# Reordering the head values by column tiles, masking keys per half, a float32 first piece of w_in, and another order of matmuls in block 1

## The chip, the cores and the metric

The kernel runs on one core of a Trainium2 chip. A core has five engines that work through their own instruction lists in order: TensorE (PE, matmuls; PEld are its weight loads), VectorE (DVE), ScalarE (ACT), GpSimd (POOL) and SyncE (SP, here only a queue that issues transfers). 16 DMA engines move data between device memory and the core's memory. The metric is device time in microseconds (us) of one execution; the median of several runs is compared.

## What is computed

Inputs are q, k, v of shape 8 x 8 x 576 x 64 (batch, heads, sequence, head width) and two weight matrices, all float32. The first stage is attention without softmax, with a decay per head, and causal; the second is a two-layer network with a hard-swish gate.

```python
scores = scale * np.matmul(q, k.transpose(0, 1, 3, 2))
gamma = 1.0 - 2.0 ** (-5.0 - np.arange(H, dtype=np.float32))
Dmat = np.where(rel >= 0, gamma[:, None, None] ** rel[None, :, :], 0.0)
attn = np.matmul(scores * Dmat[None], v)
x = attn.transpose(0, 2, 1, 3).reshape(B * S, H * D)      # 4608 x 512
h = x @ w_in                                               # 512 -> 2048
g = h * np.clip(h + 3.0, 0.0, 6.0) / 6.0
out = g @ w_out                                            # 2048 -> 512
```

## The kernel before

**Tokens and blocks.** Each of the 8 batches has 576 positions: a *head* of 64 (`TL`) and 512 (`BLK`) more. The heads of all batches together make block 0, 512 tokens; blocks 1 to 8 are the 512 later positions of each batch, in four chunks of 128 (`NCB`). Chunk number c counts from 4, so block 1 has chunks 4 to 7. There are 9 blocks (`NB`).

**Attention of a chunk.** Keys, queries and values come by SyncE's queue in float32 (`load`, L166), are cast and scaled (`casts`, L182: keys on ScalarE, queries and values on POOL) and turned on PE (`transposes`, L198; letters `c` and `t` of the plan below). Scores (`a`), products of keys and values (`s`), running state (`u`: VectorE L313 and L316, POOL L317), its cast to float16 (`z`, ScalarE L323 to L326), state times query (`x`) and scores times values (`i`) follow. The last writes PSUM, from where ScalarE copies xT, the transposed x of the block (L369).

**The network.** An up unit (`up_steps`, L491; letters L, R for the left and right half of a block's columns, U for both) makes one 128-wide slice of h from xT and a piece of w_in with four matmul steps; ScalarE makes u (L510), VectorE the gate product g (L512). Blocks 0 and 1 multiply g with w_out plainly (`down_plain`, L544; letter D is one step, 64 in a block); later blocks use a Strassen scheme, for which VectorE subtracts quarters of w_out (`weight_sums`, L644, instruction L527; letter `+`).

**Order.** Every engine's list is written by hand: the code emits instructions in the order of the function calls, and a plan string is read by `go` (L692). The tile framework adds the waits: an instruction waits on a semaphore for what it reads or overwrites.

**The heads, block 0.** The 64 head positions of a pair of batches lie as 4 (`NJ`) neighbouring positions per partition, 16 rows (`RP`) a batch. Keys and queries of head pair i are loaded in two halves (`load_half`, L390; keys of pairs 1 to 3 and all values by POOL's queue, which casts to float16 while it moves), cast on VectorE (`cast_heads`, L410) and turned on PE (`turn_heads`, L415, with the permutation `by_chunk`). Values are brought into the chunk's order by `values_heads` (L445): for each chunk four accumulated products with a sparse selection matrix `pick`, which is cleared by a POOL memset (L741) and filled by VectorE (`picks`, L431). Scores (L467) are multiplied with a mask `ws[3]` (L470), `inner_heads` (L473) multiplies them with the values and writes xT of block 0.

**The states that the heads leave.** `keys_heads` (L453) turns the head keys back on PE (hpk) and scales them by a decay on ScalarE (L458) into `kn`, which lies in the place of `ws[1]`. `head_states` (L271) multiplies `kn` with the values `vh` (in `ws[4]`) for each of four chunks; each chunk holds two batches in the two halves of its 128 rows, and each half's product is made by 64 x 64 quadrants of PE. In the plan these are `k0` to `k3` and `h0` to `h3`.

**Weights.** w_in is cut into four pieces of 512 columns, w_out into four of 512 rows; POOL's queue loads and casts them (L658, L663), after the keys and values of the heads. Up units 0 to 3 of block 0 need piece 0 of w_in, units 4 to 7 piece 1, and so on. SyncE's queue goes on with the chunks behind the third piece of w_out (`fetch(8, wout[2])`, L794).

## Time and profile before

| | us |
|---|---|
| median of 3 runs | 299.4 (299.04 to 300.53) |
| the profiled execution | 301.02 |
| its span, first to last instruction | 299.3 |
| w_in first piece landed, first up unit of block 0 | 18.0, 18.06 |
| unit 4 of block 0 | 22.27 |
| first head state on PE | 37.56 |
| chunk 4's scores | 44.98 |
| chunk 6's scores | 54.77 |
| chunk 8's scores | 67.31 |

The span covers the instructions alone; what lies around it makes the difference to the execution's time. A line of a timeline gives start, length, engine, source line, operation, tile written, tiles read and size, the number of instructions merged into it, and in brackets how long the engine had been idle before it and for whom. A matmul of 512 columns counts as busy for some 0.38 us, though the next one starts 0.11 us later. DMA shares can exceed 1, as transfers on one engine overlap.

### The profile page before, as it was taken

What the parts mean: (1) busy time and instruction counts of PE and PEld (TensorE: products, weight loads), DVE (VectorE), ACT (ScalarE), POOL (GpSimd) and SP (SyncE); (2) the same over time, 40 slices, a digit from 0 to 9 for tenths busy, and PEclk for the clock granted to TensorE, in tenths of its full rate; (3) what the DMA queues carried; (4) which work ended last, traced back from release to release, by engine and by line L of the source; (5) the groups of instructions that cost most, each with busy time, mean ns of one, the idle gap of its engine ahead of it and who ended that gap; (6) DMA issues with size and microseconds to landing.
All of it is one profiled execution on the core that took longest, in us unless ns stands there. A gap on an engine that the chain in (4) does not pass through costs nothing.

```text
span 299.3 us, 12661 instructions
## 1 busy us (share of the span) xinstructions
PE 287.4 (96%) x5574; PEld 219.3 (73%) x5574; DVE 216.2 (72%) x388; ACT 193.9 (65%) x360; POOL 133.7 (45%) x170
## 2 busy tenths in 40 slices
PE   4999998999999999999999999999999999999995
PEld 2776644777556667888777878778778987778894
DVE  7749545669897778788967797688869776647654
ACT  3748854799866696686677577667766574565420
POOL 8971057526762920719631962386247003100510
PEclk9999999999999999999999999999999999999999
DMA  6999999998999999997999999999906100200114
GB/s 157 157 182 213 186 227 209 227 228 183 161 216 164 249 202 191 178 239 195 225 220 225 169 201 216 150 177 247 148 3 142 72 2 30 102 15 2 72 72 140
DMA packets 119542, 47.86 MB, mean 160 GB/s; under 512 B 92352, under 2 KB 114880, under 8 KB 119488
## 3 DMA queue, kind: packets, MB, share of 16 engines
q1 hardware_dynamic: 114336, 41.56, 71.1%
q0 software_dynamic: 4720, 5.11, 10.5%
q8 instruction: 43, 0.70, 1.0%
q10 hardware_dynamic: 432, 0.39, 0.5%
q14 instruction: 11, 0.09, 0.1%
HBM read 36.70 MB, written 9.44 MB: 154 GB/s over the span
## 4 chain that ended last, share of the span: by engine, by line
PE 79%; DMA 9%; POOL 6%; SPq 2%; ACT 2%; issue 1%; DVE 1%; POOLq 0%; ACTq 0%
PE ph L153 37%; PE pm L153 29%; DMA wout<-in_moe_w_out_dram 6%; PE pd L153 5%; PE po L231 4%; DMA fq<-in_q_dram 2%; PE pa L231 2%; SPq L174 2%; POOL hv L439 1%; POOL hk L399 1%; POOL win L658 1%; PE pu L231 1%; POOL ws L741 1%; PE ptk L153 1%; POOL q L192 1%
## 5 line engine op out<-in xcount | busy, mean ns | idle before, releaser
L153 PE MATMUL ph<-xT,win 128*64 128x512 f16 (+1 forms) x1248 | 144.8, 364 | 1.2 <-DMA win<-in_moe_w_in_dram 0.5
L512 DVE SCALAR_TENSOR_TENSOR g<-u,ph 128x512 f16<-128x512 f32 (+1 forms) x156 | 98.8, 643 | 53.1 <-ACT u L510 52.6
L510 ACT ACTIVATE u<-ph,half 128x512 f32<-128x512 f32 (+1 forms) x156 | 100.5, 659 | 43.0 <-PE ph L153 40.6
L153 PEld LDWEIGHTS <-win 128*64 128x64 f16 x1248 | 82.9, 136 | 28.6 <-DMA win<-in_moe_w_in_dram 1.1
L153 PEld LDWEIGHTS <-g 128*64 128x64 f16 x928 | 51.1, 110 | 14.9 <-issue 0.4
L153 PEld LDWEIGHTS <-s 128*64 128x64 f16 x896 | 50.3, 110 | 8.1 <-issue 0.2
L317 POOL TENSOR_TENSOR z<-z,gpow 128x256 f32<-128x256 f32 x24 | 15.8, 657 | 69.1 <-DVE z L316 51.2
L153 PE MATMUL pm<-ws,s 128*64 128x256 f16 x672 | 45.6, 273 | 0.0
L192 POOL TENSOR_TENSOR q<-fq,dec 128x512 f16<-128x512 f32 x32 | 36.7, 1166 | 3.4 <-DVE zh L282 1.7
L369 ACT CAST xT<-po 128x256 f16<-128x256 f32 (+1 forms) x44 | 22.5, 583 | 23.4 <-PE po L231 22.5
L195 POOL TENSOR_TENSOR v<-fv,dec 128x512 f16<-128x512 f32 x32 | 35.4, 1111 | 2.1 <-DMA fv<-in_v_dram 2.1
L591 POOL TENSOR_TENSOR u<-u,p 128x512 f32<-128x512 f32 x7 | 8.9, 1271 | 60.4 <-ACT u L631 54.2
L153 PE MATMUL pd<-wout,g 128*64 128x512 f16 x256 | 34.7, 382 | 0.1
L153 PE MATMUL pm<-wout,g 128*64 128x256 f16 x448 | 31.1, 273 | 0.0
L266 DVE TENSOR_TENSOR a<-pa,mask 128x256 f16<-128x256 f32 (+1 forms) x44 | 21.9, 539 | 8.4 <-PE pa L231 4.7
L188 ACT CAST k<-fk 128x512 f16<-128x512 f32 x32 | 19.9, 622 | 2.1 <-DMA fk<-in_k_dram 2.1
L527 DVE TENSOR_TENSOR s<-g 128x1024 f16<-128x1024 f16 x28 | 19.3, 692 | 0.2
L323 ACT CAST z<-z 128x512 f16<-128x512 f32 x24 | 14.9, 622 | 5.1 <-DVE z L313 4.7
L153 PE MATMUL pm<-ws,g 128*64 128x256 f16 x224 | 16.7, 274 | 0.0
L153 PE MATMUL pm<-wout,s 128*64 128x256 f16 x224 | 16.3, 273 | 0.1
L527 DVE TENSOR_TENSOR s<-g,s 128x1024 f16<-128x1024 f16 x14 | 13.3, 949 | 0.0
L231 PE MATMUL po<-qT,z 64*64 64x64 f16 x512 | 12.5, 198 | 0.4 <-ACT z L326 0.3
(106 smaller groups left out, 270.0 us busy)
## 6 DMA issues: line engine op xcount, KB each, us to landing
fk<-in_k_dram SPq DMA_DIRECT2D x32, 256.0 KB, 4.6
fq<-in_q_dram SPq DMA_DIRECT2D x16, 512.0 KB, 6.0
fv<-in_v_dram SPq DMA_DIRECT2D x32, 256.0 KB, 5.5
out_dram<-o SPq DMA_DIRECT2D x14, 512.0 KB, 3.8
wout<-in_moe_w_out_dram POOLq DMA_DIRECT2D x4, 512.0 KB, 17.9
out_dram<-o SPq DMA_DIRECT2D x7, 256.0 KB, 5.4
win<-in_moe_w_in_dram POOLq DMA_DIRECT2D x3, 512.0 KB, 10.9
hq<-in_q_dram SPq DMA_DIRECT2D x6, 128.0 KB, 4.6
```

Of the source, the lines that this page charges most:

```text
L153: nc.tensor.matmul(out[r], lhs[:, r], rhs, skip_group_check=True, **flags)
L188: nc.scalar.copy(by_head(k16), in_rows(st[c]["fk"]))
L192: nc.gpsimd.tensor_tensor(by_head(q16[:, e]), in_rows(st[c]["fq"][:, :, e, :]), in_rows(dd[:, 2 + e, 0:H, :]), ALU.mult)
L195: nc.gpsimd.tensor_tensor(v16, st[c]["fv"], dd[:, 1, H:2 * H, :], ALU.mult)
L231: return lambda: nc.tensor.matmul(*args, skip_group_check=True, **flags)
L266: nc.vector.tensor_tensor(a16[:, a, 0:n].rearrange("p x i q -> p (x i) q"), pa[a].rearrange("p x i q -> p (x i) q"), m, ALU.mult)
L317: nc.gpsimd.tensor_tensor(new, new, decay, ALU.mult)
L323: nc.scalar.copy(z16, zs[c])
L369: nc.scalar.copy(xt[:, s], po[s].rearrange("p x n (e r) -> p x n e r", e=2))
L510: nc.scalar.activation(uu[:, 0:n], ph[:, 0:n], ACTF.Relu, bias=half, scale=1.0 / 6.0)
L512: nc.vector.scalar_tensor_tensor(out=g[:, hf, ths, jr, :], in0=by_half(uu), scalar=1.0, in1=by_half(ph), op0=ALU.min, op1=ALU.mult)
L527: nc.vector.tensor_tensor(*pend.popleft())
```

## The change

Four edits, all before the steady part of the kernel.

1. *Values of the heads.* `pick`, its memset and its four copies go. `values_heads` multiplies with 32 columns of `by_chunk` and writes each of the four neighbouring positions into its own 32 rows of the result: 16 matmuls of 32 columns a pair, no accumulation. The order of positions inside a chunk is therefore another one; keys are copied in that order by `turn_heads`, and the indices `key` and `odd` (and so the mask) follow.
2. *Keys masked per half.* As the two batches of a chunk are now interleaved in its rows, `kn` becomes two tiles, in the places of `ws[1]` and `ws[2]`: one with the second batch's rows set to zero, one with the first's. ScalarE makes one, VectorE the other, with the factors `dec_of`. `head_states` multiplies all 128 rows of each with the values.
3. *First piece of w_in.* SyncE's queue loads it in float32, in two halves behind the head queries, into a buffer `wf`; POOL casts two quarters, VectorE two. The other pieces stay on POOL's queue, with the casts of head queries 2 and 3 (moved from VectorE to POOL) ahead of and between them, and w_out's pieces behind POOL's two weight casts.
4. *Order in block 1.* The plan of block 1 runs all down steps before the first up units, turns chunk 6 behind them, and puts fewer units between the steps of chunks 6 and 7. The copies of the values, of xT and one run of idle matmuls at the start change place or number as well.

```diff
@@ -71,6 +71,7 @@
     key, odd = fj[:, 4:5], fj[:, 5:6]
     arg = const.tile([P, 4, 2 * H], FP32)
     dec = const.tile([P, 4, 2 * H], FP32)
+    dec_of = const.tile([P, 2, H], FP32)
     ident16 = const.tile([P, P], FP16)
     half = const.tile([P, 1], FP32)
     warm = const.tile([P, 1], FP32)
@@ -92,13 +93,15 @@
         nc.gpsimd.iota(query, pattern=[[TL, 2], [1, NJ], [NJ, RP]], base=0, channel_multiplier=0,
                        allow_small_or_imprecise_dtypes=True)
         make_identity(nc, ident16)
-        nc.vector.tensor_scalar(ij[:, 0:1], ii, SUB - 1, None, ALU.bitwise_and)
+        nc.vector.tensor_scalar(ij[:, 0:1], ii, RP - 1, 2, ALU.bitwise_and, ALU.logical_shift_left)
+        nc.vector.tensor_scalar(ij[:, 4:5], ii, 5, None, ALU.logical_shift_right)
         nc.vector.tensor_copy(ij[:, 1:2], ii)
         for e in range(2):
             nc.vector.tensor_scalar(ij[:, 2 + e:3 + e], ii, SUB - 1, 1, ALU.bitwise_and, ALU.logical_shift_left)
-        nc.vector.tensor_copy(ij[:, 4:5], ii)
-        nc.vector.tensor_scalar(ij[:, 5:6], ii, 6, None, ALU.logical_shift_right)
+        nc.vector.tensor_scalar(ij[:, 5:6], ii, 4, 1, ALU.logical_shift_right, ALU.bitwise_and)
         nc.vector.tensor_copy(fj, ij)
+        nc.vector.tensor_tensor(fj[:, 0:1], fj[:, 0:1], fj[:, 4:5], ALU.add)
+        nc.vector.scalar_tensor_tensor(out=key, in0=odd, scalar=float(TL), in1=fj[:, 0:1], op0=ALU.mult, op1=ALU.add)
         nc.vector.tensor_scalar(fj[:, 1:3], fj[:, 1:3], 1.0, -float(P // 2), ALU.mult, ALU.add)
         nc.vector.tensor_scalar(fj[:, 3:4], fj[:, 3:4], 1.0, 1.0 - float(P // 2), ALU.mult, ALU.add)
         nc.vector.tensor_copy(by_chunk.rearrange("p (c e r) -> p c e r", c=NCB, e=2),
@@ -123,6 +126,8 @@
             nc.gpsimd.tensor_scalar(arg[:, :, h], fj[:, 0:4], lg, float(np.log(D ** -0.5)), ALU.mult, ALU.add)
             nc.gpsimd.tensor_scalar(arg[:, :, H + h], fj[:, 0:4], -lg, 0.0, ALU.mult, ALU.add)
         nc.scalar.activation(dec, arg, ACTF.Exp)
+        nc.gpsimd.tensor_scalar(dec_of[:, 1, :], dec[:, 0, H:2 * H], odd, None, ALU.mult)
+        nc.gpsimd.tensor_tensor(dec_of[:, 0, :], dec[:, 0, H:2 * H], dec_of[:, 1, :], ALU.subtract)
 
     def decays_of_chunk():
         for h in range(H):
@@ -270,14 +275,12 @@
 
     def head_states(c):
         pu = [psum.tile([P, NP, D], FP32, tag="pp", name=f"pu{e}_{c}") for e in range(2)]
-        todo = ([], [])
         for i in range(NP):
-            for a in range(2):
-                j, h2 = divmod(i + NP * a, 2)
-                for e in range(2):
-                    todo[e].append(mm(pu[e][rows(a), i], kn[rows(e), j, c, h2 * D:h2 * D + D],
-                                      vh[rows(e), c, j, h2, :], start=True, stop=True))
-        in_turn(todo)
+            for e in range(2):
+                for a in range(2):
+                    j, h2 = divmod(i + NP * a, 2)
+                    nc.tensor.matmul(pu[e][rows(a), i], kn[e][:, j, c, h2 * D:h2 * D + D], vh[:, c, j, h2, :],
+                                     start=True, stop=True, skip_group_check=True)
         nc.scalar.copy(zh[c + NCB], pu[1])
         nc.vector.tensor_tensor(zh[c], pu[0], decay, ALU.mult)
         nc.gpsimd.tensor_tensor(zh[c + NCB], zh[c + NCB], decay, ALU.mult)
@@ -379,7 +382,7 @@
 
 
     hd = {}
-    kn = ws[1].rearrange("p j n -> p (j n)").rearrange("p (i c x) -> p i c x", i=NP, c=NCB)
+    kn = [ws[n].rearrange("p j n -> p (j n)").rearrange("p (i c x) -> p i c x", i=NP, c=NCB) for n in (1, 2)]
     vh = ws[4].rearrange("p j n -> p (j n)").rearrange("p (c i e d) -> p c i e d", c=NCB, i=NP, e=2)
 
     def after(i, behind):
@@ -423,39 +426,46 @@
         if nm == "q":
             copy(t.rearrange("p (x j r) -> p x j r", j=NJ, r=RP), pt.rearrange("p j (x r) -> p x j r", r=RP))
         else:
-            copy(t.rearrange("p (x r j) -> p x r j", j=NJ, r=RP), pt.rearrange("p j (x r) -> p x r j", r=RP))
+            copy(t.rearrange("p (c j y) -> p c j y", c=NCB, j=NJ), pt.rearrange("p j (c y) -> p c j y", c=NCB))
         hd[i][nm + "T"] = t.rearrange("p (c y) -> p c y", c=NCB)
 
-    pick = ws[2].rearrange("p j n -> p (j n)").rearrange("p (j c m) -> p j c m", j=NJ, c=NCB)
-
-    def picks():
-        for j in range(NJ):
-            nc.vector.tensor_copy(pick[:, j].rearrange("p c (x j) -> p (c x) j", j=NJ)[:, :, j], by_chunk)
-
-    def load_values(i, behind=None):
-
-        t = heads16(i, "v")
+    def load_pair(i, nm, behind=None):
+
+        t = heads16(i, nm)
         for e in range(2):
             d = nc.gpsimd.dma_start(t[:, e].rearrange("p j d -> p (j d)"),
-                                    v[:, 2 * i + e, 0:TL, :].rearrange("b (r j) d -> r b (j d)", j=NJ))
+                                    dict(k=k, v=v)[nm][:, 2 * i + e, 0:TL, :].rearrange("b (r j) d -> r b (j d)", j=NJ))
             if behind is not None:
                 after(d, behind)
-        hd.setdefault(i, {})["v"] = t
+        hd.setdefault(i, {})[nm] = t
 
     def values_heads(i, copy):
 
         pv = psum.tile([P, NCB, 2, D], FP32, tag="st", bufs=2, name=f"hpv{i}")
+        m = P // NJ
         for c in range(NCB):
             for j in range(NJ):
-                product(pv[:, c], pick[:, j, c, :], hd[i]["v"][:, :, j, :], start=(j == 0), stop=(j == NJ - 1))
+                nc.tensor.matmul(pv[m * j:m * j + m, c], by_chunk[:, m * c:m * c + m], hd[i]["v"][:, :, j, :],
+                                 start=True, stop=True, skip_group_check=True)
         copy(vh[:, :, i], pv)
+
+    wf = gp.tile([P, NP, BLK], FP32, tag="g", bufs=4, name="wf")
+
+    def load_win():
+        for i in range(2):
+            nc.sync.dma_start(wf[:, 2 * i:2 * i + 2], win_v[:, 2 * i:2 * i + 2, 0:BLK])
+
+    def cast_win(i, copy):
+        copy(win16[0][:, i], wf[:, i])
 
     def keys_heads(i):
         pk = psum.tile([P, NCB, 2, D], FP32, tag="pp", name=f"hpk{i}")
         for c in range(NCB):
             product(pk[:, c].rearrange("p a d -> p (a d)"), hd[i]["kT"][:, c, :], ident16, start=True, stop=True)
         for a in range(2):
-            nc.scalar.mul(kn[:, i, :, a * D:a * D + D], pk[:, :, a, :], dec[:, 0, H + 2 * i + a:H + 2 * i + a + 1])
+            nc.scalar.mul(kn[0][:, i, :, a * D:a * D + D], pk[:, :, a, :], dec_of[:, 0, 2 * i + a:2 * i + a + 1])
+            nc.vector.tensor_scalar(kn[1][:, i, :, a * D:a * D + D], pk[:, :, a, :], dec_of[:, 1, 2 * i + a:2 * i + a + 1], None,
+                                    ALU.mult)
 
     def scores_heads(i):
         kT, qT = hd[i]["kT"], hd[i]["qT"]
@@ -734,38 +744,34 @@
         for i in (2, 3):
             for e in range(2):
                 load_half(i, "q", e, sp, keys)
+        load_win()
         for i in (1, 2, 3):
-            for e in range(2):
-                load_half(i, "k", e, pool, None if i == 1 else keys)
-            if i == 1:
-                nc.gpsimd.memset(pick, 0.0)
+            load_pair(i, "k", None if i == 1 else keys)
         for i in range(NP):
-            load_values(i)
-        win_piece(0, 2)
-        for n in (1, 2, 3):
-            win_piece(n)
-        wout = [wout_piece(pc) for pc in (0, 2, 1, 3)]
+            load_pair(i, "v")
         distances()
         idle_products(5)
         mask_of_heads(0)
         cast_heads(0, "k", on_dve)
-        picks()
         turn_heads(0, "k", on_act)
         mask_of_heads(1)
-        idle_products(4)
+        idle_products(3)
         cast_heads(0, "q", on_dve)
         mask_of_heads(2)
         turn_heads(0, "q", on_act)
         cast_heads(1, "q", on_dve)
         turn_heads(1, "k", on_act)
         turn_heads(1, "q", on_act)
-        cast_heads(2, "q", on_dve)
+        cast_heads(2, "q", pool.tensor_copy)
+        win_piece(1)
+        cast_heads(3, "q", pool.tensor_copy)
+        for n in (2, 3):
+            win_piece(n)
         scores_heads(0)
         mask_of_heads(3)
         idle_products(1)
         turn_heads(2, "k", on_act)
         turn_heads(2, "q", on_act)
-        cast_heads(3, "q", on_dve)
         scores_heads(1)
         idle_products(1)
         turn_heads(3, "k", on_act)
@@ -774,11 +780,16 @@
         values_heads(0, on_act)
         scores_heads(3)
         values_heads(1, on_act)
-        inner_heads(0, on_act)
-        values_heads(2, on_dve)
+        inner_heads(0, on_dve)
+        values_heads(2, on_act)
         inner_heads(1, on_dve)
         values_heads(3, on_act)
-        inner_heads(2, on_dve)
+        for i in range(2):
+            cast_win(i, pool.tensor_copy)
+        wout = [wout_piece(pc) for pc in (0, 2, 1, 3)]
+        for i in (2, 3):
+            cast_win(i, on_dve)
+        inner_heads(2, on_act)
         first = [up_steps(0, u) for u in range(4)]
         for dmc in range(3):
             for unit in first:
@@ -797,8 +808,8 @@
         weight_sums(3)
         weight_sums(1, 2, 4)
         down = down_plain(0)
-        go("k0 D4 k1 D4 +1 k2 D4 +1 k3 D6 h0 D2 c4 h1 D3 h2 D3 h3 D3 D4 c5 t4 D5 a4 s4 u4 D5 z4 t5 c6 D4 "
-           "x4 a5 s5 i4 u5 z5 D5 t6 x5 D2 i5 D4 L2 c7 a6 s6 u6 L3 z6 D1 t7 L3 x6 a7 s7 i6 u7 D1 L1 z7 L2 c8 L1 D2 x7 D1 i7 t8 D3 "
+        go("k0 D4 k1 D4 +1 k2 D4 +1 k3 D6 h0 D2 c4 h1 D3 h2 D3 h3 D7 c5 t4 D4 a4 s4 u4 D4 z4 t5 c6 D4 "
+           "x4 a5 s5 i4 u5 z5 D5 x5 D4 i5 D10 L2 t6 L2 c7 a6 s6 u6 L1 z6 t7 L2 x6 a7 s7 i6 u7 L1 z7 L2 x7 L1 c8 i7 L1 t8 "
            "R3 c9 R3 a8 s8 u8 R2 t9 z8 R4 c10 x8 a9 s9 i8 u9 U1 z9 c11 t10 U3",
            1, down)
         down = down_plain(1)
```

## The prediction

> **What bounds the kernel now.** I read the page first, then the busy time by stage, then the timeline of the first 60 us, engine by engine, and last what DMA moved around the first weights.
>
> ```profile
> span 299.3 us, 12661 instructions
> PE 287.4 (96%) x5574; PEld 219.3 (73%) x5574; DVE 216.2 (72%) x388; ACT 193.9 (65%) x360; POOL 133.7 (45%) x170
> ```
> ```profile
> 10.00:22.00 12.00, 11.67 (x262) 8.98 (x260) 7.25 (x12) 6.68 (x15) 10.34 (x29) 1.00 1.09 156
> 22.00:37.00 15.00, 14.73 (x160) 9.49 (x162) 11.21 (x17) 12.90 (x25) 1.15 (x12) 1.00 1.04 199
> 37.00:67.00 30.00, 27.30 (x640) 18.80 (x637) 17.49 (x41) 20.61 (x49) 16.21 (x19) 1.00 1.03 222
> 90.00:294.00 204.00, 203.73 (x3876) 163.06 (x3874) 151.88 (x251) 130.04 (x224) 81.43 (x77) 1.00 0.76 144
> ```
> The columns of the second fence are the stretch, its length, then PE, PEld, DVE, ACT, POOL busy, granted clock, DMA share, GB/s. From 90 to 294 us PE rests 0.27 us of 204. So whatever PE has gained or lost by 90 us stands in the end one for one. All edits lie before 70 us, and the question is only how PE's place in its own list moves there.
>
> ```profile
> 11.65 3.84 POOL L658 DMA_DIRECT2D win<-in_moe_w_in_dram  x5
> 12.93 1.08 PE L153 MATMUL hpv<-hv,ws 128*64 128x128 f16 x32
> 18.06 1.95 PE L153 MATMUL ph<-xT,win 128*64 128x512 f16 x16 [0.25 <-DMA win<-in_moe_w_in_dram]
> 22.27 10.58 PE L153 MATMUL ph<-xT,win 128*64 128x512 f16 x96 [0.28 <-DMA win<-in_moe_w_in_dram]
> 33.48 1.56 ACT L458 ACTIVATE ws<-hpk,dec 128x256 f16<-128x256 f32 x4
> 33.62 0.69 DVE L512 SCALAR_TENSOR_TENSOR g<-u,ph 128x512 f16<-128x512 f32 x1 [0.17 <-ACT u L510]
> 37.56 0.21 PEld L231 LDWEIGHTS <-ws 64*64 64x64 f16 x16 [0.41 <-ACT ws L458]
> 37.78 0.69 DVE L527 TENSOR_TENSOR ws<-wout 128x1024 f16<-128x1024 f16 x1 [2.87 <-DMA wout<-in_moe_w_out_dram]
> 48.90 0.41 DVE L313 TENSOR_TENSOR z<-pa,z 128x256 f32<-128x256 f32 x1
> 49.34 0.62 ACT L323 CAST z<-z 128x512 f16<-128x512 f32 x1
> 50.42 0.41 PE L153 MATMUL ptq<-ident,q 128*64 128x128 f16 x8 [0.63 <-POOL q L192]
> 51.42 0.41 PE L153 MATMUL ptq<-ident,q 128*64 128x128 f16 x8 [0.59 <-POOL q L192]
> ```
> Three places matter. At 18.06 and 22.27 the first block's up units wait for pieces of w_in. At 37.56 the first head state (L231, pu) waits 0.41 us for ScalarE's scaled keys. At 50 to 52 us PE waits twice for POOL's queries of chunk 6.
>
> **The front, 0 to 22 us.** *Removed:* the memset of the pick tile on POOL (3.02 to 4.86) and VectorE's four copies into it. The third keys DMA is issued only when the memset ends; its order needs just SyncE's first keys, issued at 0.82 and 3.0 us to landing, so 3.8. POOL's row of key and value issues moves up 0.9: the next instruction stands at 10.75 instead of 11.65. *Moved to POOL:* the casts of query pairs 2 and 3. No row has such a cast there. From below, a quarter of the memset of 2048 columns (1.84 us) is 0.46; from above, the two-input product of the same tile is 1.17 (L192). I take 0.8, the middle. (The Trainium skill, GPSIMD Engine Reference, section Elementwise, puts 512 elements of a tight loop at 769 ns; by it the sum below stays within 0.1.) Pair 2 is ready at 10.75 + 0.8 = 11.55; then comes the issue of w_in's second piece (starts 0.73 apart, 12.38 to 13.09 among the w_in issues), then pair 3, ready at 13.1. Behind these on POOL stand two w_in pieces (14.5), two casts of the first piece (16.1), then w_out's four issues.
>
> PE, in its fixed list, turns pair 2's queries at 11.6 (10.76 before) and pair 3's at 13.15 (12.26 before). *Saved:* the values take 64 matmuls of 32 columns instead of 128; at the old pitch (12.93 to 13.95 for 32, 0.032 each) 0.5 us a pair instead of 1.02, so 2.1 in all. At half that pitch it would be 3.1, but ScalarE's copies of 0.58 each then set the pace. VectorE ends the masked scores (0.69 each, the last pair of them at 16.5) and copies xT of pair 0 until 17.2: the first up unit starts at about 17.3, not 18.06. VectorE's two weight casts (0.43 each, as L412) end at 18.8, ahead of the third step at 19.6. Four units with the last heads' product take 3.85: unit 4 starts at 21.15 instead of 22.27. **A lead of 1.1**, if w_in's second piece has landed. Its bound is DMA: between 12 and 16 us the software queue kept the 16 engines busy to 91.4% for 0.43 MB, between 18 and 22 to 122.1% for 0.80 MB, so the float32 piece on SyncE's queue (issued from 6.35, 1 MB) has a gap to fill; I put the landing at 20.2, bounds 18.7 and 22.2 (no gain). The lead lies between 0 and 1.5. The index arithmetic (three more VectorE steps of 0.15) hides before the keys land; uncovered, 0.4.
>
> **The keys, 32 to 40 us.** Before, ScalarE alone makes eight scaled copies (0.47 each by L458's group), ending at 37.2. Now each has a twin on VectorE from the same PSUM tile. In the order of the built program the two do not run side by side: VectorE's copy waits for ScalarE's of the same half, and ScalarE's second half waits for VectorE's first. VectorE's 128x256 from PSUM takes 0.42 (L282). Also VectorE's queue holds the two weight sums of 0.69 (L527) behind pairs 1 and 2, so pairs 2 and 3 stand behind them, and the second sum also needs the last piece of w_out (37.7 before). In old clock: last gate product ends 34.31; pair 0 on VectorE to 34.73; ScalarE's second half to 35.23; then VectorE's second half beside ScalarE's next first half to 35.7. One pair thus costs 0.42 + 0.47 + 0.42 + hand-overs of 0.03 (u ends 29.27, g starts 29.30), or 1.4. Pairs 1, 2, 3 end at 37.10, then with the sums 39.17 and 41.27. PE's first head state needs all four pairs: its end goes from 37.8 to 41.4, **3.6 later** by itself. Bounds: VectorE's copies at 0.3 and ScalarE's at 0.42 give 2.6; 0.1 more on each give 4.6. With the lead it stands at 40.3, so PE is then 2.5 behind.
>
> *Head states:* 16 matmuls each as before, but two 64-column tiles instead of four quadrants. Old pitch 0.24 for 16; eight of 128 columns took 0.22 (hpk), so at most 0.44. Four times 0 to 0.2; I take **0.3**.
>
> **Block 1, 41 to 67 us.** The same work in another order: all 64 down steps come first, t6 is moved behind them, fewer fillers stand between chunks 6 and 7. *Gone:* the two waits of 0.63 and 0.59, one of 0.49 for chunk 4's query, one of 0.39 for gate products and one of 0.42 for xT; each loses some 0.2 more than its row, since a matmul's own 0.2 to 0.4 is counted as busy: 3.5. *New,* from the chain of a state: masked scores start on PE at 47.72, z is cast at 49.96, 2.24 later. x5 has only five down steps before it (1.6 with the scores): 0.65. x6 has three up units and t7 (2.0): 0.6 with VectorE's gate products in the way. x7: 0.5. Chunk 6's scores follow t6 after two up units (1.4 with t6) while VectorE copies both queries (0.69 each behind a gate product, 2.25): 0.9. An up unit right behind i6 and i7 waits for ScalarE's xT copies: 0.4 as before, and at i7 1.6 (0.76 for two copies, 0.62 for a keys cast in the queue, 0.2), where t8 and three down steps stood. Sum 4.7. **Net 1.2 later**, bounds 0 and 2.3.
>
> **Sum.** -1.1 + 3.6 + 0.3 + 1.2 = **+4.0**. The profiled run took 301.0 with a span of 299.3; it would be a span of 303.3 and a time of 305.0. That run lay 1.6 above the median shown, so the median goes from 299.4 to **303.4**.
>
> **Rivals.** *A, no lead:* w_in's second piece lands at 22.2 as before; all else the same, 304.5. For it: DMA share is over 1 in all of 10 to 37 us. (The Trainium skill, DMA: Bandwidth & Descriptors, section "Issuing engines are not separate DMA queues", says that queues share the same 16 engines, so another queue adds no transfer rate.) Against it: the gap at 12 to 16. *B, the key copies run side by side:* VectorE alone still needs 8 x 0.42 + 2 x 0.69 = 4.7 from 34.31, to 39.05; that costs 1.35 instead of 3.6: 301.2. For it: both only read the tile. Against it: the waits in the program. *C, not slower:* the new order of block 1 takes away all 3.5 and nothing comes in their place, since moving t6 frees PE from POOL and from the load of chunk 6: -1.1 + 3.6 + 0.3 - 3.5 = -0.7, 298.7. It decides as soon as the new waits stay under some 2 us in total. Against it: state chains of 2.24 with covers of 1.6 to 2.0. *D:* B and C together, 296.5; here the keys' turn would have to be hidden too.
>
> **How the numbers follow.** Forecast 0.60, A 0.18, B 0.10, C 0.08, D 0.04. A measurement tells about 0.5% (1.5 us) from no change, so 297.9 to 300.9 is the same. B splits evenly between same and slower: faster 0.04, same 0.13, slower 0.83. The range reaches from 300.3 (halfway into B; cheaper copies and a cheap block 1) to 305.4 (A with a dearer block 1 or a POOL cast of 1.17, which costs 0.7); the likeliest case's own range is 301.5 to 305.
>
> **What would show it.** After: POOL casts of about 0.8 and PE waiting for them near 10 to 13 us; unit 4 at about 21; ScalarE and VectorE copies of hpk in turns, and PE loads of ws waiting in pieces near 36 to 40 for a sum of 3 us or more; waits for xT and z at 57 to 68; from 90 us on PE without gaps, some 4 us later in its list. A head state that starts whole before 38 refutes the main step; chunk 8's scores before 68 (67.3 now) refute the sum.

## The result and the profile after

The changed kernel takes 311.1 us (median of four, 308.7 to 311.3), before it 299.3 in the same job: 1.037 times as long, 95% interval 1.031 to 1.043. The forecast was 303.4. The direction was right; 7.7 us are missing from the sum. Three slow runs below (738 us in e1, 582 in the traced run of e3_keysplit, 303.6 in c4) are left out of the ratios.

The page of the changed kernel, its span and busy times:

```profile
span 306.6 us, 12542 instructions
PE 287.0 (94%) x5508; PEld 223.0 (73%) x5508; DVE 214.9 (70%) x393; ACT 195.3 (64%) x361; POOL 132.2 (43%) x173
```

TensorE (PE) is busy for as long as before (287.4 us), though it has 66 matmuls fewer: the span has grown by rests. Three stretches of it (columns as in the prediction: from:to, length, PE, PEld, DVE, ACT, POOL busy, granted clock, DMA share, GB/s):

```profile
9.00:12.00 3.00, 1.81 (x26) 1.00 (x21) 1.29 (x2) 2.00 (x5) 2.13 (x5) 0.51 1.10 245
12.00:16.00 4.00, 3.39 (x58) 2.39 (x58) 1.44 (x3) 1.66 (x3) 3.60 (x6) 0.52 1.24 265
90.00:294.00 204.00, 200.77 (x3868) 157.99 (x3866) 151.35 (x251) 131.62 (x228) 81.28 (x78) 1.00 0.78 143
```

Two things are new. From 9 to 16 us the granted clock is halved, and from 90 to 294 us TensorE rests 3.2 us where it rested 0.27. The front in TensorE's timeline (start, duration, group, what it waited for), with one line of POOL's queue between:

```profile
7.71 0.41 PE L422 MATMUL hptq<-by_chunk,hq 128*64 128x128 f16 x8 [1.57 <-DVE hq L415]
9.62 0.52 POOL L436 DMA_DIRECT2D hv<-in_v_dram  x1 [1.17 <-DMA hk<-in_k_dram]
12.61 0.64 PE L422 MATMUL hptq<-by_chunk,hq 128*64 128x128 f16 x8 [1.80 <-POOL hq L415]
18.99 1.95 PE L158 MATMUL ph<-xT,win 128*64 128x512 f16 x16 [0.29 <-DVE xT L491]
```

Eight matmuls of a turn take 0.41 at 7.71, behind a rest of 1.57, and 0.64 at 12.61; the recorded clock is halved from 9.0 to 15.9. POOL rests 1.17 before its fifth issue of values, so the cast of query pair 2, for which TensorE waits until 12.61, starts only at 11.90. The first up unit starts at 18.99 (18.06 before), unit 4 at 22.69 (22.27). The keys, on ScalarE, VectorE and TensorE:

```profile
38.59 0.84 ACT L466 ACTIVATE ws<-hpk,dec_of 128x256 f16<-128x256 f32 x2 [1.18 <-DVE ws L467]
39.09 0.48 DVE L467 TENSOR_SCALAR ws<-hpk,dec_of 128x256 f16<-128x256 f32 x1 [0.54 <-ACT ws L466]
39.49 0.68 DVE L537 TENSOR_TENSOR ws<-wout 128x1024 f16<-128x1024 f16 x1
40.62 0.22 PE L282 MATMUL pu<-ws,ws 128*64 128x64 f16 x2 [0.74 <-DVE ws L467]
41.65 0.22 PE L282 MATMUL pu<-ws,ws 128*64 128x64 f16 x1 [0.30 <-DVE ws L467]
```

ScalarE waits for VectorE and VectorE for ScalarE, a weight sum of 0.68 stands between, and the first head state ends at 41.86 instead of 37.88. And the rests behind 90 us, all of this stretch that the profile marks "issue" (nothing that it shows was waited for):

```profile
143.09 0.28 PE L236 MATMUL po<-qT,z 64*64 64x64 f16 x9 [0.52 <-issue]
162.68 0.63 PE L158 MATMUL pm<-wout,s 128*64 128x256 f16 x8 [0.63 <-issue]
173.67 0.22 PE L236 MATMUL po<-a,v 64*64 64x64 f16 x2 [0.26 <-issue]
206.66 0.52 PE L158 MATMUL pm<-wout,g 128*64 128x256 f16 x5 [0.73 <-issue]
218.95 0.25 PE L236 MATMUL po<-a,v 64*64 64x64 f16 x6 [0.58 <-issue]
```

They sum to 2.72. Counted in TensorE's instruction list, each falls on the 194th or 195th instruction of a group of 256. The page's queue 8, "instruction", makes 43 transfers of 0.70 MB in all, 16 KB each; TensorE's list has some 11,040 instructions, about 256 for each transfer. Each rest ends 2.4 to 2.8 us after such a transfer began. A boundary between two such pieces of the list is called a joint below.

How far each trace is behind the trace of the kernel before, in us, at four places (a unit is taken at the start of its `u` on ScalarE; these columns count units from one, so unit 8 is the eighth):

| kernel | block 0, unit 8 | end of first head state | block 1, unit 15 | end of span |
|---|---|---|---|---|
| changed | 0.46 | 3.98 | 4.43 | 7.34 |
| forecast | -1.1 | 2.5 | 4.0 | 4.0 |

### The profile page after: what moved, and what is told of

Its sections match the earlier page's. It is cut to its first block, busy times and chain, and to the rows that moved or that the text cites. A ratio compares the mean times of both kernels' runs of the same rounds, so it can differ in the third digit from the quotient of the medians.

```text
span 306.6 us, 12542 instructions
## 1 busy us (share of the span) xinstructions
PE 287.0 (94%) x5508; PEld 223.0 (73%) x5508; DVE 214.9 (70%) x393; ACT 195.3 (64%) x361; POOL 132.2 (43%) x173
## 4 chain that ended last, share of the span: by engine, by line
PE 85%; DVE 4%; ACT 4%; DMA 3%; issue 2%; POOL 1%; DVEq 0%; ACTq 0%
PE ph L158 40%; PE pm L158 28%; PE pd L158 7%; PE po L236 4%; DMA hk<-in_k_dram 3%; PE pa L236 3%; PE pu L236 1%; ACT u L520 1%; DVE ws L467 1%; DVE qT L216 1%; DVE g L522 1%; PE ptk L158 1%; POOL hv L436 1%; ACT ws L466 1%; ACT kT L216 1%
## 5 line engine op out<-in xcount | busy, mean ns | idle before, releaser
L158 PEld LDWEIGHTS <-win 128*64 128x64 f16 x1248 | 86.1, 136 | 26.0 <-issue 2.2
L158 PEld LDWEIGHTS <-g 128*64 128x64 f16 x928 | 52.3, 110 | 15.4 <-issue 1.4
L271 DVE TENSOR_TENSOR a<-pa,mask 128x256 f16<-128x256 f32 (+1 forms) x44 | 21.9, 539 | 7.7 <-PE pa L236 5.0
L236 PEld LDWEIGHTS <-z 64*64 64x64 f16 x512 | 8.0, 106 | 8.0 <-issue 2.6
```

Source lines behind the costliest of these rows:

```text
L158: nc.tensor.matmul(out[r], lhs[:, r], rhs, skip_group_check=True, **flags)
L236: return lambda: nc.tensor.matmul(*args, skip_group_check=True, **flags)
L271: nc.vector.tensor_tensor(a16[:, a, 0:n].rearrange("p x i q -> p (x i) q"), pa[a].rearrange("p x i q -> p (x i) q"), m, ALU.mult)
```

## The experiments

Ratios are to the kernel before in the same job, with 95% intervals. A lag compares one execution with one, and executions of one kernel differ: the kernel before took 298.5 to 302.8 us in the 80 runs beside these experiments. The theories A to E of the expectations are other ones than the rivals A to D of the prediction. The same four lags for all traces that are used below:

| run | unit 8 | head state | unit 15 of block 1 | end | ratio |
|---|---|---|---|---|---|
| changed, again (after_b) | 1.20 | 4.71 | 8.43 | 11.80 | 1.036 (1.030 to 1.042) |
| e1_pad132 | -0.13 | 3.44 | 6.53 | 6.90 | 1.023 (1.018 to 1.028) |
| e2_oldplan | 2.63 | 6.15 | 3.29 | 6.46 | 1.021 (1.015 to 1.027) |
| e3_keysplit_b | 1.03 | 2.08 | 2.53 | 6.05 | 1.018 (1.014 to 1.023) |
| e5_front | -0.47 | 3.05 | 3.49 | 6.75 | 1.034 (1.026 to 1.041) |
| e7_win16 | 0.37 | 3.89 | 5.96 | 8.80 | 1.029 (1.026 to 1.033) |
| d1_busy | -0.39 | 3.17 | 5.09 | 7.66 | 1.032 (1.027 to 1.037) |
| e8_front_both | 0.58 | 4.11 | 4.56 | 7.89 | 1.030 (1.026 to 1.035) |
| b1_pad124 | -0.49 | 0.46 | 1.51 | 4.58 | 1.008 (1.005 to 1.011) |
| c1_masked_values | -0.18 | -0.22 | -3.09 | -2.87 | 0.9974 (0.9945 to 1.0003) |
| c1_again | 1.05 | 1.00 | -1.86 | -1.67 | 0.9997 (0.9971 to 1.0023) |
| c2_filled | 1.76 | 1.72 | -1.04 | 1.14 | 1.003 (1.000 to 1.006) |
| c3_filled_newplan | 0.00 | -0.05 | 0.41 | 1.94 | 1.013 (1.009 to 1.017) |
| c4_gated | 1.34 | 1.30 | -1.33 | -1.00 | 1.0005 (0.9976 to 1.0033) |
| c5_win16 | -0.90 | 0.25 | -2.62 | -2.54 | 0.9968 (0.9940 to 0.9996) |

**The rests behind 90 us: e1_pad132 and b1_pad124.** One puts the number of TensorE instructions back in the changed kernel, the other (with p31 for p33) shifts the list of the kernel before as the change does.

```
+    def pad(n):
+        idle = psum.tile([P, NP, P], FP32, tag="pp", name="pad")
+        for _ in range(n):
+            product(idle[:, 0, 0:1], ident16, ident16[:, 0:1], start=True, stop=True)
-  k3 D6 h0 D2 c4
+  k3 D6 p33 h0 D2 c4
```

> The changed kernel with 33 one-column products of the identity (66 matmuls and 66 weight loads, 132 TensorE instructions) put in front of the first head state, where TensorE waits for the keys; nothing else differs and their result is not read. Theory A (TensorE's instructions come in pieces of 256, and the change, which has 132 fewer of them, has moved the joints between pieces to places where the next piece comes too late): with the old places of the joints the five stalls after 142 us go; TensorE is busy 203.5 us or more of 90 to 294 instead of 200.8, the lag against the kernel before stays at what it is at 90 us, and the median falls from 311.1 by some 2.7 to 308.4, less whatever of the products (about 1.5 us by themselves) the wait for the keys does not hide. Rival (the stalls come from DMA traffic, or are chance): stalls of 2 to 3 us in sum stay, at these or other places, and the median is 311 to 313.

> The kernel before with 31 one-column products (124 TensorE instructions) in front of the first head state, so that every later instruction stands in its 256-piece where it stands in the changed kernel. Theory A (joints of the pieces): the stalls of the changed kernel appear after 140 us at the same groups of matmuls, 2 to 3 us in sum, and the median is 299.4 + 2.7 + up to 1.5 for the products themselves: 302 to 303.5. Rival (the stalls belong to something else in the change): TensorE stays without gaps from 90 to 294 us, and the median is 299.4 to 301.

The kernel before with 124 more instructions, its "issue" rests from 90 us on:

```profile
139.92 0.28 PE L231 MATMUL po<-qT,z 64*64 64x64 f16 x9 [0.26 <-issue]
159.50 0.63 PE L153 MATMUL pm<-wout,s 128*64 128x256 f16 x8 [0.52 <-issue]
171.05 0.22 PE L231 MATMUL po<-a,v 64*64 64x64 f16 x2 [0.81 <-issue]
203.78 0.52 PE L153 MATMUL pm<-wout,g 128*64 128x256 f16 x5 [0.46 <-issue]
216.07 0.25 PE L231 MATMUL po<-a,v 64*64 64x64 f16 x6 [0.58 <-issue]
```

The same five groups, down to the count of matmuls behind each rest, 2.63 us in sum, in a kernel that otherwise is the one before; from unit 15 of block 1 to the end it loses 3.1 us. The changed kernel with 132 more, on the other hand:

```profile
90.00:294.00 204.00, 202.96 (x3920) 158.81 (x3922) 153.83 (x253) 132.88 (x231) 83.87 (x79) 1.00 0.82 148
```

It loses 0.37 us there instead of 2.9. One rest of 0.35 is left, at another joint. So the joints of the instruction pieces cause the rests: shown in both directions. In every other trace, too, the rests marked "issue" behind 90 us fall on the 194th or 195th instruction of a group of 256. Which joints stall is not a matter of the place alone: d1_busy, 24 instructions longer than the changed kernel, had two rests (1.76 and 1.08), and c2_filled, only eight shorter than c1_masked_values, lost 2.2 us there against 0.2. In the traces the transfer of the next piece starts between 1.9 us before and 3.7 us after a joint, and a rest follows where the 256 instructions up to the next joint run out sooner than some 2.4 us after that start. What delays the start is open.

**The keys: e3_keysplit and e3_keysplit_b** (one kernel, run twice; the trace is of the second).

```
-        for a in range(2):
-            nc.scalar.mul(kn[0][...], pk[:, :, a, :], dec_of[:, 0, ...])
-            nc.vector.tensor_scalar(kn[1][...], pk[:, :, a, :], dec_of[:, 1, ...], None, ALU.mult)
+        for a in range(2):
+            for x in range(2):
+                if i % 2:
+                    nc.vector.tensor_scalar(kn[x][...], pk[:, :, a, :], dec_of[:, x, ...], None, ALU.mult)
+                else:
+                    nc.scalar.mul(kn[x][...], pk[:, :, a, :], dec_of[:, x, ...])
```

> The changed kernel with the scaled key copies shared by pair instead of by half: ScalarE makes all four copies of pairs 0 and 2, VectorE all four of pairs 1 and 3. The number of copies, their sizes and TensorE's list stay. Theory B (the two engines work in turns on one tile and so cost some 3.5 us): the tiles are now copied side by side; VectorE needs 4 x 0.48 + 2 x 0.69 = 3.3 from its last gate product at 34.7, so the last head state's matmuls go at about 38.3 instead of 41.65, and the median falls by some 3.2 to 308. Rival (the copies are not the bound; the sums of weights, which wait for the pieces of w_out, or TensorE's own work are): the head states end after 40.5 and the median falls by less than 1.2. Second rival (the gain is given back in block 1, which waits for chunks 4 to 7): head states at 38.3 but chunk 8's scores still after 71, and a median of 311.

> The key copies shared by pair, once more, for a trace. Theory B: the last head state's matmuls end at about 38.5 instead of 41.65 with TensorE waits of under 1 us in front of them, the half clock after 37 us does not come, and the median is 305 to 307, that is 4 to 6 under the changed kernel. Rival: head states after 40.5; then the gain of the first run of this kernel came from the clock alone.

TensorE's first head state there:

```profile
38.96 0.22 PE L282 MATMUL pu<-ws,ws 128*64 128x64 f16 x2 [0.17 <-DVE ws L469]
39.35 0.22 PE L282 MATMUL pu<-ws,ws 128*64 128x64 f16 x2 [0.17 <-DVE ws L469]
39.75 0.22 PE L282 MATMUL pu<-ws,ws 128*64 128x64 f16 x1 [0.17 <-DVE ws L469]
```

With as many copies of the same size, three waits of 0.17 are left of six that summed to 2.4. From unit 8 to the head state this kernel loses 1.05 us; the eight traces with the keys of the change lose 3.5 to 3.6 each. The turns cost 2.5 us, shown; the ratio falls from 1.037 to 1.018 (and 1.017 in the first run), more than 2.5 us; the next paragraph has a reading of the rest.

**The changed kernel again, and what the keys' waits do to the clock.**

> The changed kernel once more, for a second trace. Theory A (joints of instruction pieces): TensorE stalls again at the same groups of matmuls after 140 us (po<-qT,z, pm<-wout,s, po<-a,v, pm<-wout,g, po<-a,v), none before that from 90 us on. Theory C (clock): the granted clock is about 0.5 for some 7 us after the waits of 7 to 13 us, or after those of 37 to 41 us. Rival (chance): the stalls stand at other groups. Time 309 to 311.5.

The five rests come back at the same groups (0.32, 0.73, 1.14, 0.73, 0.21). From head state to unit 15 of block 1 this trace loses 3.7 us, the first one 0.45. Its windows there:

```profile
42.00:44.00 2.00, 1.70 (x29) 1.09 (x29) 1.08 (x3) 1.17 (x3) 0.84 (x2) 0.84 0.94 211
44.00:46.00 2.00, 2.00 (x31) 1.33 (x29) 0.42 (x1) 0.37 (x1) 2.00 (x3) 0.50 1.27 299
46.00:48.00 2.00, 2.00 (x31) 1.32 (x29) 0.42 (x1) 0.96 (x2) 2.00 (x4) 0.80 1.26 216
```

The clock is halved right behind the keys' waits, recorded from 43.4 to 46.8, and once more from 70.7 to 74.1, behind the new order's wait of 1.15 for xT; against the first trace the first stretch costs 1.6 us and the second 1.7. Of eight traces with the keys in turns, four show a half clock at or behind the keys' waits (after_b, e1, e7, d1) and lose 1.9 to 3.7 us between these two places; the three others with the same order of block 1 lose 0.44 to 0.45. e3_keysplit_b, with most of the waits gone, and the six traces of the masked-values versions, which do not wait at the keys, do not show it at that place. That short waits close together bring a stretch of half clock, in some executions and not in others, is a reading of these traces; no run filled the waits alone.

**The order of block 1: e2_oldplan, and c3_filled_newplan beside c2_filled.**

```
-  ... h3 D7 c5 t4 D4 a4 s4 u4 D4 z4 t5 c6 D4 x4 a5 s5 i4 u5 z5 D5 x5 D4 i5 D10 L2 t6 L2 c7 a6 s6 u6 L1 z6 t7 L2 ...
+  ... h3 D3 D4 c5 t4 D5 a4 s4 u4 D5 z4 t5 c6 D4 x4 a5 s5 i4 u5 z5 D5 t6 x5 D2 i5 D4 L2 c7 a6 s6 u6 L3 z6 D1 t7 L3 ...
```

> The changed kernel with block 1 in the order of the kernel before (its first list of steps put back); all else as changed. Theory D (the new order costs what the prediction's net 1.2, bounds 0 to 2.3, says; the lag grows from 2.4 us at block 1's first up unit to 4.4 at 75 us in the trace): the lag at 75 us falls to 2.5 to 3.5, the median by 1 to 2, to 309 to 310. Rival 1 (the lag grows there because of the late keys and the late loads alone): lag 4.4 stays, median 311. Rival 2 (the new order gains for a state that is late): median 312 or more.

> The same with block 1 in the new order. Theory D (the new order costs some 2 us also when the heads' states are early): median 1.5 to 2.5 over that of the version with the old order; waits of TensorE for the queries of chunk 6 and for xT at 56 to 68 us as in the changed kernel. Rival (the new order was made for an early state and gains there): same or less.

The same stretch in the changed kernel, then with the old order:

```profile
44.00:75.00 31.00, 26.99 (x654) 20.45 (x652) 18.25 (x46) 22.73 (x52) 14.87 (x19) 1.00 0.84 185
```
```profile
44.00:75.00 31.00, 29.71 (x728) 22.66 (x727) 20.64 (x52) 24.81 (x60) 17.60 (x21) 1.00 0.86 184
```

With the old order TensorE gets through 74 matmuls more in these 31 us. From head state to unit 15 it does not lose 0.45 but gains 2.86 on the kernel before, as c1 (2.87), c2 (2.76), c4 (2.62) and c5 (2.87) do; with the new order c3 loses 0.46 again, in a state that is early. So the new order costs 3.2 to 3.3 us against the old in these traces, whether the state is late or early; by the medians of one job, c3 stands 2.5 us over c2. Its waits are the same in c3 and in the changed kernel. The longest, an up unit behind i7 that waits for xT, in the changed kernel:

```profile
59.51 0.32 PE L236 MATMUL pa<-qT,kT 64*64 64x64 f16 x16 [0.74 <-DVE qT L216]
67.97 0.55 PE L158 MATMUL ph<-xT,win 128*64 128x256 f16 x6 [1.15 <-ACT xT L372]
```

and in c3_filled_newplan:

```profile
55.48 0.32 PE L235 MATMUL pa<-qT,kT 64*64 64x64 f16 x16 [0.74 <-DVE qT L215]
63.95 0.55 PE L157 MATMUL ph<-xT,win 128*64 128x256 f16 x6 [1.15 <-ACT xT L371]
```

Why the old order gains on itself: TensorE's three waits for POOL's queries, 1.7 us in sum before, are gone in e2, c1 and c5. That earlier loads bring this was only argued: the loads of chunk 4 start at 33.1 us in the changed kernel, 33.8 in c5 and 35.2 before, since they wait for a piece of w_out that lands earlier, and chunk 6's queries land at 49.2 before, at 45.6 in e2 and 46.5 in c5. No run moved the loads alone.

**The front: e5_front, e7_win16, d1_busy, e8_front_both.** The first puts the casts of query pairs 2 and 3 back on VectorE, with one idle product more; the second the first piece of w_in back on POOL's queue in float16; the third fills TensorE's rests (six idle products ahead of the first queries, three ahead of those of pair 2); the fourth is the first with the float32 piece held back until the first values have landed.

```
e5   -  cast_heads(2, "q", pool.tensor_copy)  ...  idle_products(3)
     +  cast_heads(2, "q", on_dve)            ...  idle_products(4)
e7   -  load_win()  ...  cast_win(i, pool.tensor_copy)  ...  cast_win(i, on_dve)
     +  win_piece(0, 2)
d1   -  idle_products(3)
     +  idle_products(6)  ...  idle_products(3)
e8   -  nc.sync.dma_start(wf[:, 2 * i:2 * i + 2], ...)
     +  after(nc.sync.dma_start(wf[:, 2 * i:2 * i + 2], ...), came[0, "v", 1])
```

> The changed kernel with the casts of query pairs 2 and 3 back on VectorE where they were, and four idle products instead of three; the float32 piece of w_in, the values and all behind them as changed. Theory C (TensorE waits 3.8 us for POOL's casts and for the keys, its clock is halved for that, and the lead of the front is lost so): the granted clock stays at 1.0 from 9 to 16 us, the values are then ready earlier, and the first up unit starts at 17.5 to 18 instead of 18.99; the lag at unit 4 falls by 0.5 to 1.4, the median to about 310. Rival (the landing of the values at 17.5 or of the float32 piece at 16.3 with its casts sets the first up unit): clock better or not, the first up unit stays at 18.8 or later and the median at 311.

> The changed kernel with the first piece of w_in back on POOL's queue in float16 (two parts, behind the cast of query pair 3), without SyncE's float32 transfers and the four casts of it; all else as changed. Theory E (the float32 piece on SyncE's queue takes the DMA engines from the values, which therefore land at 17.5 to 19 us instead of 14.4, and so the front has no lead): the values land by 14.5 to 15.5, TensorE never waits for them, the piece of w_in lands at 18 to 19.5 as before and then sets the first up unit, at 18.1 to 18.6; the lag against before at the eighth unit is 0 to 0.4 (0.46 to 2.6 in the three traces with the changed front). The median falls by 0.3 to 1.5. Rival (TensorE's half clock and the wait for POOL's casts set the front): first up unit at 18.9 or later although the values are there, median 311.

> The changed kernel with idle products in TensorE's first waits: six instead of three ahead of the first queries, and three more ahead of the queries of pair 2 (24 TensorE instructions more). Theory C (a matmul of the front takes 1.5 times as long for some 7 us after TensorE has rested for 1.5 us): with the rests filled the eight products of a turn take 0.41 from 9.5 us on, the granted clock is not lowered between 9 and 16, and the first up unit goes as soon as the last values have landed, 18.2 to 19.2; median 309 to 310.5. The clock may still fall after the keys' wait at 38 to 41 us. Rival (the clock falls for another reason, or its fall costs nothing since the values land late anyway): clock of 0.5 as before, or none and first up unit and median unchanged at 18.9 to 20.5 and 311.

> The changed kernel with both causes of the front taken away: the casts of query pairs 2 and 3 back on VectorE and four idle products, and the two float32 transfers of w_in on SyncE's queue start only when the first pair's values have landed (about 11.4 us). If theories C and E together are the whole of the lost lead: the values land by 14 to 15.5, TensorE rests less than 0.8 us in sum between 9.5 and 17, w_in's piece lands at 16.5 to 17.5, the first up unit starts at 17.3 to 18.0 and the lag against before at the eighth unit is -0.6 to -1.2 (the forecast's lead); later as the changed kernel (keys +3.5, order +2, joints +2 to +3), median 308 to 309.5. Rival (the engines' transfers are the bound: what the values gain the float32 piece loses): first up unit at 18.4 or later, lag at the eighth unit -0.4 or more.

The last values land at 14.36 us before, 17.47 in the changed kernel (19.04 in its second trace), 17.28 in e5, 13.45 in e7, 13.99 in e8. So the float32 piece does take the engines from the values, as theory E says. In the first trace of the changed kernel TensorE came too late itself to wait for them; in the second it did wait:

```profile
19.18 0.41 PE L448 MATMUL hpv<-hv,by_chunk 128*32 128x128 f16 x16 [1.05 <-DMA hv<-in_v_dram]
```

But taking the piece away alone does not start the first up unit earlier: in e7 it starts at 18.95, since TensorE still waits 1.60 for POOL's cast and its eight products take 0.6 until 17.4. In e5 and d1 the products are fast from 11.5 or throughout, the up units start at 18.09 and 18.07, and TensorE waits for values instead (0.72 and 1.41 in e5). And with both causes gone, e8:

```profile
17.34 1.95 PE L158 MATMUL ph<-xT,win 128*64 128x512 f16 x16 [1.08 <-POOL win L461]
21.08 2.16 PE L158 MATMUL ph<-xT,win 128*64 128x512 f16 x18 [1.57 <-DVE win L461]
```

Now TensorE is done with the values, and with the third pair's product, at 16.26 and waits for the float32 piece, whose halves land at 16.62 and 20.57. The first up unit comes at 17.34, where the theory put it, but the lag at unit 8 (0.58) is the rival's: the values and the piece share the transfers, and whichever goes first, the other is late. The four medians (ratios 1.029 to 1.034) lie at or just under the changed kernel's. Theory C is borne out in part. With the rest ahead of the first queries cut from 1.57 to 0.60, d1 has the fast products, in one trace. But c2_filled, where rests of the front were filled too, showed the half clock at 18.5 to 21.9 us and a mean clock under 0.995 in nine of twelve runs. And the slow products of e5 and e7 are no fall of the clock: its record shows the first rise only at 11.5 and 17.8 us there.

**Versions that leave out what cost: c1_masked_values, c2_filled, c4_gated, c5_win16.** c1 is the changed kernel with e5's front, its idle products cut in four (the old number of TensorE instructions to within four), the old order of block 1, and the values' halves (vh, vo) masked instead of the keys, during block 0's units 6 to 12:

```
+        nc.vector.tensor_scalar(dst, src, (even, odd)[e], None, ALU.mult)
+            if i % 2:
+                nc.vector.tensor_scalar(kn[...], pk[:, :, a, :], d, None, ALU.mult)
+            else:
+                nc.scalar.mul(kn[...], pk[:, :, a, :], d)
```

c5 is c1 with the transfers of w_in and w_out as in the kernel before, without the float32 piece; c2 is c1 with more idle products, most of them cut in two only; c4 is c1 with the float32 piece held back as in e8.

> A version built of what the runs so far point to: the changed front with the casts of queries 2 and 3 back on VectorE and four idle products, all idle products in four column pieces each (132 more TensorE instructions, so the joints of the 256-pieces stand after the values as in the kernel before); the values' parity halves instead of the keys are masked, by VectorE from SBUF to SBUF during block 0's up units 6 to 12; the scaled keys once each, pairs 0 and 2 by ScalarE, 1 and 3 by VectorE; block 1 in the old order. Theories A to D together: clock 1.0 all through, no stalls after 90 us, unit 7 some 0.4 us ahead of the kernel before, the first head state at 37.0 to 37.6 (VectorE's 34.0 + 4 x 0.48 + 2 x 0.69), and the median of before minus 0.3 to 0.8. If one of them is wrong: stalls after 140 us (A) 2 to 3 more, a half clock (C) 2 to 3 more, head states after 39 (B) 1.5 to 3 more.

> The version with masked values, with its waits of the front filled: six idle products instead of four ahead of the first queries, and two each ahead of the first and second pair's values. Theory C: the half clock, which showed as a mean clock of 0.986 to 0.994 in seven of ten runs of that version (spans 297.4 to 300.7) and not in three (296.4, 297.4, 298.1), goes: all runs at 0.998 or more, median 297.5 to 299, 2 to 3 under the kernel before in the same job. Rival: the clock does not depend on these waits; median 299.9 again or, by the added products, 300.

> The version with masked values, with the float32 transfers of w_in started only when the first pair's values have landed. If TensorE's rests of 1.39 and 1.08 us for the values made the half clock: clock 0.998 or more in nearly all runs and a median of 296.5 to 298.5, 2 to 4 under the kernel before. Rival 1 (w_in's piece now lands too late): first up unit after 18.8, median 300 or more. Rival 2 (the clock falls for the rests at 4 to 8 us): clocks of 0.986 to 0.994 in most runs again and a median of 299 to 300.5.

> The version with masked values once more, beside the gated one and the kernel before in one job: median 299 to 300.5, 0.5 to 1.5 us under the kernel before.

> The version with masked values, with the front's w_in and w_out transfers as in the kernel before (first piece in float16 on POOL's queue behind the values, then the others), so without the float32 piece and its casts. If the half clock of the front comes of the rests for the values: clock 1.0 in nearly all runs, the eighth unit at -0.5 to +0.3 against before, and then the gain of block 1 either stays (it came with the keys and values: -1.5 to -3 at block 1's fifteenth unit, median 296.5 to 298) or goes (it came with the loads, which the float32 piece made 2 us earlier: 0 to -1, median 298.5 to 299.5). Rival: clock of 0.986 to 0.994 in most runs and 300 as without this.

c1 came to 299.9 us against 300.8 (0.997), and to 300.0 against 300.0 when run again (1.000, interval 0.997 to 1.002); c4 to 300.3 (1.0005, 0.998 to 1.003); c2 to 302.0, slower by its joints and its late front. c5 takes 299.6 against 300.6: 0.997, interval 0.994 to 0.9996, the only version whose interval stays under 1; among five such comparisons that is weak evidence of a gain. Its first up units:

```profile
16.25 1.95 PE L157 MATMUL ph<-xT,win 128*64 128x512 f16 x16 [0.65 <-DMA win<-in_moe_w_in_dram]
21.38 1.95 PE L157 MATMUL ph<-xT,win 128*64 128x512 f16 x16 [1.19 <-DMA win<-in_moe_w_in_dram]
```

It leads the kernel before by 0.90 at unit 8, near the lead that was forecast for the change, with the values in their new order and without the float32 piece. What sets this lead is w_in's second piece, for which TensorE has waited 1.19: it lands at 21.33 instead of 22.23. The gain of block 1 stays (0.25 to -2.62), so it does not need that piece either.

## Why the forecast fell short

*The front, forecast -1.1, measured 0.46.* Three steps failed. "POOL's row of key and value issues moves up 0.9: the next instruction stands at 10.75" did not hold: with the rest of 1.17 it stood at 11.90, so TensorE turned pair 2's queries at 12.61 instead of 11.6. POOL's cast itself takes 0.66 where 0.8 was taken. The sum also held the matmul rates of the old front, while the clock was halved from 9.0 to 15.9, behind TensorE's rests of 1.57 and 0.46. And "the float32 piece on SyncE's queue has a gap to fill" looked at the wrong landing: its bounds were set on w_in's second piece, which came at 19.99, as put (20.2); what came late was the values, by 3.1 us. In the first trace the first two steps hide this; with the casts back on VectorE (e5) the front leads by 0.47, short of 1.1 with 2.1 us of waits for values. Rival A had this end ("no lead") by another cause.

*The keys, forecast 3.6, measured 3.5.* Mechanism and size hold: in turns, with both weight sums in between. Rival B (side by side) falls.

*Head states and block 1, forecast 0.3 + 1.2, measured 0.45 together.* The net is within its bounds, but one reading in it is wrong: the 3.5 us of old waits were booked as a gain of the new order. They go with the old order too, by 2.6 to 2.9 us net; the new order merely has 3.2 to 3.3 us of new waits in their place (4.7 were forecast). Rival C, which let all waits go, had the right gain and the wrong order. That the lag at unit 15 (4.43) came so near the forecast (4.0) is luck: the front is 1.6 worse and block 1 1.1 better than put.

*From 90 us on, forecast nothing, measured 2.9.* This is the step "whatever PE has gained or lost by 90 us stands in the end one for one". It took an instruction list with 132 entries fewer to be as good as the old one. The Trainium skill, Runtime: NRT & Kernel Launch, section "Instruction fetch mechanics", states that instructions stream in blocks of 16 KiB (256) and that crossing a boundary is mostly hidden; the trace agrees on the block (43 transfers of 16 KB), and the five rests of 0.26 to 0.73 here were not hidden.

*From span to median, forecast -1.6, measured +2.4.* The step "that run lay 1.6 above the median shown" carried over an offset from three runs. It did not hold even for the kernel before: the 80 runs beside the experiments have a median of 300.7, 0.3 under its profiled 301.0. The profiled run of the changed kernel (308.7) is its shortest of six. Its second trace is 4.5 us longer: 0.7 in the front, 3.3 at the two stretches of half clock, 0.5 at the joints. The other runs left no trace, and their recorded mean clocks do not follow the times (308.7 us at 0.988, 311.1 at 1.000).

So of the 7.7 us missing, 1.5 come of the front, -1.1 of block 1 and the keys, 2.9 of the joints: together 3.3, the difference between the lags 7.3 and 4.0. Of the remaining 4.4, the step from profiled run to median makes 4.0, and the time stands 0.4 further above the span than before. Some 1.3 of the 4.0 is the low median of the kernel before's first three runs (299.4 against 300.7). The rest stays open: the second trace points at the clock, but one trace does not prove it for the median.

## What to carry over

A transfer moved to another queue to fill a gap has to be priced on what is in flight beside it, not only on its own landing: ask which load lands later. Where an edit removes waits, ask whether they would go anyway with the other edits in place, and try the old order with them. Removing instructions ahead of a long instruction stream moves every later joint of 256; compare such kernels with the old count padded in before a late loss is laid at anything else. A step from one profiled run to a median needs more than three runs behind it.

## What had not been expected of the hardware

The joints: up to 1.76 us at one of them (d1_busy, 161.0 to 162.8), and 2.6 to 3.5 us from block 1 to the end in the nine traces whose list is shorter by 108 to 132 or longer by 124, against 0.1 to 0.4 in five with the old count or four more (e1, c1 twice, c4, c5). Two with four fewer lost 2.2 and 1.5 (c2, c3).

The clock: a stretch of 6.8 us at half (9.0 to 15.9) behind rests of 1.6 and 0.5 us, and others of 3.4 or 6.8 us at or behind six waits of 0.28 to 0.74 within four. The Trainium skill, TensorE: Matmul & The Clock Gate, section "Part 1: The HAM clock gate (the "warmup" mystery)", gives an idle window of about 3.4 us that runs freely as the condition for half rate; here no single rest of TensorE was longer than 1.94 us, and the fall came in some executions and not in others. On the free-running window the traces agree: in each, all recorded changes of the clock lie whole multiples of 3.41 us apart (in after_b 5.83, 9.24, 16.07, 43.38, 46.79), and where they lie differs from trace to trace.

The start: the record of the clock begins with a first rise, at 5.1 to 21.9 us (9.7 in the kernel before), and matmuls ahead of it run at half rate: in the kernel before, pairs of the 128-column ones start 0.107 us apart ahead of 9.7 and 0.056 behind. In e2_oldplan, where it comes last, eight matmuls of a turn take 0.64 instead of 0.41 from 7.3 to 20 us, and its front is the latest of all (2.63). The windows show 1.00 there, since nothing is recorded, so a mean clock of 1.00 does not exclude a slow start: the matmuls' own times are the better witness.
